# The attention of a chunk queued one slot later, from the fifth chunk on, in a linear-attention kernel followed by a gated feed-forward block

## The chip, the cores and the metric

The kernel runs on one core of a Trainium2 chip. The metric is device time in microseconds (us) of one execution, the median of several. Engines are named as in the profile: PE (TensorE, with its weight loads PEld), DVE (VectorE), ACT (ScalarE), POOL (GpSimd) and SP (the queue that issues most of the transfers).

## The reference

Queries, keys and values have shape (8 batches, 8 heads, 576 positions, 64), and `omega` maps 64 to 128 features. The result of the attention, 4608 tokens of 512 numbers, goes through two products that are multiplied element by element, and two more products.

```python
def phi(x):
    proj = np.einsum('bhsd,md->bhsm', x, omega)
    h = proj - np.sum(x * x, axis=-1, keepdims=True) / 2.0
    h = h - np.max(h, axis=-1, keepdims=True)
    return np.exp(h) / np.sqrt(m)
q_p, k_p = (phi(q * scale), phi(k * scale))
kv = np.einsum('bhsm,bhsd->bhmd', k_p, v)
z = np.sum(k_p, axis=2)
num = np.einsum('bhsm,bhmd->bhsd', q_p, kv)
den = np.einsum('bhsm,bhm->bhs', q_p, z)[..., None] + 1e-06
x = (num / den)          # then as 4608 x 512
a, b = x @ w1, x @ w2
out = (a * b @ w3) @ w_out
```

## The kernel before, in words

The tokens are cut into 36 chunks of 128, all heads together. A batch is 4.5 chunks long, so some chunks hold rows of two batches. Nearly every product is done in float16 with each operand split into a high and a low part, three matmuls in place of one (`PASSES`); a split costs one instruction for the high part and one for the low part, on two engines as the letters `KS`, `QS`, `VS`, `EH`, `EL`, `QH`, `QL` say.

What is done for one chunk of queries `c`, and where:

- `load`: SP fetches `qraw` and `kraw` (two buffers each).
- `norm` and `scale`: ACT sums squares (L153), PE adds them over partitions (`norm_q_k`, L158), DVE makes scales of them (L168 to L227).
- `split_raw`: ACT (L136) and DVE (L139) make `qhl`, `khl`; then the load of the chunk after next is issued.
- `features`: 24 PE matmuls into a PSUM tile `qpj` (or `kpj` for keys; L254); DVE finds the row maximum `nm` (L259) and subtracts it, `qe` (L267); ACT takes the exponential (L268).
- `q_chunk` (L337 on): after `features`, DVE casts the high part `eq` (L125), POOL makes the low part (L277), and SP issues two transposing transfers `eqT<-eq` (L344). `eqT` has two buffers, `eq` has one.
- `k_chunk` runs five chunks ahead (`LEAD`), with `ek` in place of `eq` and no transposition. When the last chunk of a batch has its `ek`, `kv_batch` runs 120 matmuls into `kvp` (L322), which ACT and DVE evict (L331, L332).
- Values: once for a batch, PE adds squares (`norm_v`), then POOL makes five high parts `vhl` (L138) and DVE five low parts (L139). These are called batch-of-values work below.
- `q_attend` (L346 on): 24 matmuls into a PSUM tile `nu` (L357; 48 of half the height where a chunk holds two batches), then DVE divides: `gd`, `gr`, `xs`, `mx` (L366 to L379).
- `ready`, with `x_turn` in it: DVE and ACT split the result, `xhl` (L393, L394), SP transposes it into `xT` (L398), and the units of the feed-forward block that need it are put in a queue.

The feed-forward units are `gate` (48 matmuls of 256 columns for a pair of chunks, L581, or 96 of 128 columns for each of the first four chunks; ACT, DVE and POOL turn them into two halves of `h`) and `project_out` (24 matmuls of 512 columns, L607; ACT scales it, L611, SP stores it). Each `project_out` also has a small DVE instruction `osc` (L603), whose four buffers come free when the ACT instruction of four units before is done. Three units belong to each chunk: two of `gate`, one of `project_out`.

Two PSUM pools matter. `ps_a` has two buffers of two banks, and `qpj`, `kpj`, `nu` and `kvp` take them in turn, in the order in which the Python code asks for them (function `banks`). `ps_m` has four buffers of one bank for everything else.

The order of the work comes from numbered slots. `step(i)` puts the parts of chunk `i` into slots with `put(slot, rank, fn)`; a chunk begins every three slots, at `at0`. At the end of the program one loop goes through the slots. In each slot it runs first a share of the work on the weights, then at most one unit of the feed-forward queue (above slot 40, `EAGER`, only if the queue holds more than two, `RESERVE`), then the parts put into the slot by rank, then one piece of work on values. Within that order a list scheduler places the instructions on each engine: an instruction that cannot start yet by its estimate lets later ones pass. Each engine runs its own list in order. Chunk `i` has its query and key features in slot `at0` (ranks 1 and 2), and before the change its attention in `at0 + 2` and `ready` in `at0 + 3`.

The weights (stored in 64 bits) are converted in the first 240 us or so, while the first chunks go through; this stretch is not repeated.

Of the kernel before, what the change touches and what calls it, by code (L numbers as in the profile page):

```python
# [47 lines left out]
GROUPS = [(0, 1), (1, 1), (2, 1), (3, 1)]  # L48
RESERVE = 2
EAGER = 40  # L50
RAW64_BUFS = 3
O_BUFS = 3
RAW_BUFS = 2
# [10 lines left out]
def tile_favor_attention_then_bilinear_ffn(  # L64
# [42 lines left out]
    def banks(name):  # L107
        return ps_a.tile([P, 2, 512], F32, tag="pa", name=name)
# [4 lines left out]
    def small(name, n=1, rows=P, dt=F32, bufs=4):  # L113
        return sm.tile([rows, n], dt, tag=f"s_{name}", name=name, bufs=bufs)
# [126 lines left out]
    def place(h):  # L241

        return h % 2 * NP + h // 2
# [102 lines left out]
    def q_attend(c):  # L346

        t = eqs.pop(c)
        owners = [
            (b, max(b * S - c * P, 0), min((b + 1) * S - c * P, P))  # L350
            for b in range(c * P // S, ((c + 1) * P - 1) // S + 1)
        ]
        nu = banks(f"nu_{c}")[:, :, 0 : 4 * E].rearrange("p g (i e) -> p g i e", e=E)
        for h in range(H):
            for b, r0, r1 in owners:
                for n, (x, y) in enumerate(PASSES):
                    nc.tensor.matmul(  # L357
                        nu[r0:r1, h // 4, h % 4],
                        t[:, x, place(h), r0:r1],
                        kvs[b][:, y, h],  # L360
                        start=n == 0,
                        stop=n == 2,
                    )

        gd = small("gd", H)
        nc.vector.tensor_scalar_add(  # L366
            gd.rearrange("p (g i) -> p g i", g=2), nu[:, :, :, D], 1e-6 * M * 2.0**21
        )
        gr = small("gr", H)
        nc.vector.reciprocal(gr, gd)  # L370
        xs = at.tile([P, HD], F32, tag="xs", name=f"xs_{c}", bufs=1)
        nc.vector.tensor_tensor(
            xs.rearrange("p (g i d) -> p g i d", g=2, d=D),
            nu[:, :, :, 0:D],
            gr.rearrange("p (g i) -> p g i", g=2).unsqueeze(3).broadcast_to([P, 2, 4, D]),
            ALU.mult,
        )
        mx = small("mx")
        nc.vector.tensor_reduce(mx, xs, AX.X, ALU.max, apply_absolute_value=True)  # L379
        xss[c] = xs, mx, owners  # L380

    def x_turn(c):

        xs, mx, owners = xss.pop(c)
        nc.vector.tensor_scalar(mx, mx, TINY, 2.0**-12, ALU.max, ALU.mult)
        p, r = pow2(mx, 1, f"x{c}")

        pt = sm.tile([P, 1], F32, tag="pt", name=f"pt_{c}", bufs=14)
        for b, r0, r1 in owners:
            nc.vector.tensor_scalar(pt[r0:r1], p[r0:r1], pv[b][r0:r1], None, ALU.mult)  # L390
        pts[c] = pt
        t = at.tile([P, 2, HD], F16, tag="xhl", name=f"xhl_{c}", bufs=1)
        nc.scalar.mul(t[:, 0], xs, r)  # L393
        nc.vector.scalar_tensor_tensor(t[:, 1], xs, r, t[:, 0], ALU.mult, ALU.subtract)  # L394
        mc, off = c * P // TOK, c * P % TOK
        if mc not in xT:
            xT[mc] = at.tile([P, 2, NC, TOK], F16, tag="xT", name=f"xT_{mc}", bufs=XT_BUFS)
        nc.sync.dma_start_transpose(  # L398
            xT[mc].rearrange("p x c s -> p (x c) s")[:, :, off : off + P],
            t.rearrange("p x d -> p (x d)"),  # L400
        )
# [16 lines left out]
    arena = const.tile([P, ARENA, 512], F32, name="arena")  # L418
    raw_at = list(range(0, 4 * RAW64_BUFS, 4))
    mag_at = list(range(4 * RAW64_BUFS, 4 * RAW64_BUFS + 4, 2))  # L420
    free = list(range(4 * RAW64_BUFS + 4, ARENA))

# [145 lines left out]
    def gate(c0, n, u):  # L568

        nf, T = 4 // n, n * P  # L570
        x = xT[c0 * P // TOK]
        off = c0 * P % TOK
        ab = []
        for m in range(2):
            ps = bank_m(f"ab_{c0}_{u}_{m}").rearrange("p (f s) -> p f s", f=nf)
            for k in range(nf):
                f = u * nf + k
                i, r = f // (NF // 2), f % (NF // 2)
                mm = [(cc, a, b) for cc in range(NC) for a, b in PASSES]
                for j, (cc, a, b) in enumerate(mm):  # L580
                    nc.tensor.matmul(  # L581
                        ps[:, k],
                        w12[m][i][cc][:, a, r * P : (r + 1) * P],
                        x[:, b, cc, off : off + T],
                        start=j == 0,
                        stop=j == len(mm) - 1,
                    )
            ab.append(ps)
        asb = mo.tile([P, nf, T], F32, tag="asb", name=f"asb_{c0}_{u}", bufs=ASB_BUFS)
        nc.scalar.mul(asb, ab[0], 2.0**-37)  # L590
        nc.vector.tensor_tensor(asb, ab[1], asb, ALU.mult)  # L591
        place = block()
        left[place] = nf * n
        h = arena[:, place].bitcast(F16).rearrange("p (x f s) -> p x f s", x=2, f=nf)
        nc.gpsimd.tensor_scalar(h[:, 0], asb, 1.0, 1.0, ALU.mult, ALU.mult)  # L595
        nc.gpsimd.tensor_tensor(h[:, 1], asb, h[:, 0], ALU.subtract)  # L596
        for k in range(nf):
            for t in range(n):
                hs[c0 + t, u * nf + k] = h[:, :, k, t * P : (t + 1) * P], place

    def project_out(c):
        sc = small("osc")
        nc.vector.tensor_scalar(sc, pts[c], pts[c], kap, ALU.mult, ALU.mult)  # L603
        ps = bank_m(f"o_{c}")
        mm = [(f, a, b) for f in range(NF) for a, b in PASSES]
        for i, (f, a, b) in enumerate(mm):
            nc.tensor.matmul(ps, hs[c, f][0][:, a], W[f][:, b], start=i == 0, stop=i == len(mm) - 1)  # L607
        for f in range(NF):
            used(hs[c, f][1])
        o = mo.tile([P, DO], F32, tag="o", name=f"o_{c}", bufs=O_BUFS)  # L610
        nc.scalar.mul(o, ps, sc)  # L611
        nc.sync.dma_start(out[c * P : (c + 1) * P, :], o)
# [15 lines left out]
    def v_unit(n=1):  # L628
        for x in v_work[:n]:
            x()  # L630
        del v_work[:n]
# [51 lines left out]
    def put(slot, rank, fn):  # L683
        plan.setdefault(slot, []).append((rank, len(plan[slot]) if slot in plan else 0, fn))
# [3 lines left out]
    def ready(c):  # L688
        x_turn(c)
        for c0, m in groups:  # L690
            if c0 + m == c + 1:
                units = []
                for u in range(2 * m):
                    need = [(n, u // m) for n in range(2)]
                    units.append((need, lambda c0=c0, m=m, u=u: gate(c0, m, u)))

                for k, f in enumerate(behind_by):
                    units.insert(2 + 3 * k, f)
                behind_by[:] = [(["k"], lambda c=c: project_out(c)) for c in range(c0, c0 + m)]
                queue.extend(units)  # L700
                if c + 1 == NCH:
                    queue.extend(behind_by)

    def step(i):
        at0 = begin[i]
        kc = i + LEAD
        keys = [(n, c) for n, c in (("q", i), ("k", kc)) if 0 <= c < NCH]
        state = {}

        def norms():  # L710
            state["am"] = norm(keys, i)

        def splits():
            for name, c in keys:
                split_raw(c, name)
                if c + 2 < NCH:
                    load(srcs[name], c + 2, name)

        put(at0 - 3, 3, norms)
        put(at0 - 2, 6, lambda: scale(keys, state["am"]))  # L720
        put(at0 - 1, 8, splits)
        if i >= 0:
            put(at0, 1, lambda: q_chunk(i))
            put(at0 + 2, 7, lambda: q_attend(i))
            put(at0 + 3, 0, lambda: ready(i))
        if kc < NCH:
            put(at0, 2, lambda: k_chunk(kc))
        if kc in B_OF_K:

            def kv():  # L730
                v_unit(len(v_work))
                kv_batch(B_OF_K[kc])

            put((begin[i + 1] if i + 1 in begin else at0 + 3) - 1, 5, kv)
        for b in range(B):
            cs = [c for c, _, _ in chunks_of(b)]
            if cs[1] == kc:
                put(at0, 9, lambda b=b: v_batch(b))
            if cs[0] == kc:
                put(at0 + 2, 10, lambda cs=cs: [v_load(c) for c in cs if c not in vraw])  # L740
# [7 lines left out]
    for t in range(max(plan) + 1):  # L748
        n = min(PER[t] if t < len(PER) else 1, len(ticks))
        weights(n)  # L750
        if not ticks and raw_at:
            for a, w in [(a, 4) for a in raw_at] + [(a, 2) for a in mag_at]:
                free.extend(range(a, a + w))
            raw_at.clear()
        unit(RESERVE if t > EAGER else 0)
        for _, _, fn in sorted(plan.get(t, []), key=lambda x: x[:2]):
# [43 lines left out]
```

## Time and profile before

| | |
|---|---|
| median of 3 runs | 932.87 us (929.71 to 1192.34) |
| the profiled execution, its own time | 932.87 us |
| its span in the trace | 931.1 us |
| PE busy | 809.9 us, 87% |
| PEld / DVE / ACT / POOL busy | 64% / 68% / 44% / 35% |
| waits of PE at `nu` for the transposed features `eqT`, 312 to 876 us | 26.3 us in 15 waits |

How to read it: the span is covered by PE for 87%, so a microsecond taken from another engine shows in the time only where PE waits for it. One run of the three shown is far above the others, and the median is the run that was profiled. The 1.8 us between the span and the time lie around the span.

In the rows of the timeline the columns are: start, length, engine, line, operation, tile written and tiles read, matmul shape, count, and in brackets the idle time of the engine before it and what ended it.

### The profile page before, as it was taken

The page shows a single profiled execution, that of the slowest core. Times are in us where ns is not written, and L with a number is a line of the kernel's source. Part 1 is how long each engine was busy: PE and PEld are TensorE (multiplying, and loading weights), DVE is VectorE, ACT ScalarE, POOL GpSimd, SP SyncE. Part 2 cuts the span into 40 slices and gives each one's busy share as a digit, 9 for nine tenths or more (in the row PEclk, how much of TensorE's full clock was granted, in tenths as well). Part 3 has the DMA queues.
Part 4 walks back from the last instruction along what each step waited for, and adds up shares of the span by engine and source line. Part 5 has one row for each costly group of instructions (what it writes and reads, how often), then busy time and mean ns, then how long its engine had stood idle before and what let it go on. Part 6 is the DMA issues. An engine that isn't in the chain of part 4 may idle for free.

```text
span 931.1 us, 20482 instructions
## 1 busy us (share of the span) xinstructions
PE 809.9 (87%) x8593; PEld 598.3 (64%) x8598; DVE 637.7 (68%) x1119; ACT 406.9 (44%) x695; POOL 324.7 (35%) x317
## 2 busy tenths in 40 slices
PE   1964397689996998999989998989899989999998
PEld 1433253577775766777757766767577757777774
DVE  5779789889787478667876787566857875556210
ACT  3587764556435343444344533444354333322111
POOL 0000004232454256433543464343533643423311
PEclk9985599689998799999989998999899989999999
DMA  8445455332444145333432343243423422333200
GB/s 312 163 137 181 136 148 178 83 70 59 92 114 83 43 91 126 92 70 81 114 80 69 80 125 80 65 96 79 115 71 69 69 59 58 74 76 58 46 24 34
DMA packets 142524, 88.42 MB, mean 95 GB/s; under 512 B 116704, under 2 KB 116832, under 8 KB 142432
## 3 DMA queue, kind: packets, MB, share of 16 engines
q1 hardware_dynamic: 134944, 66.15, 30.1%
q10 hardware_dynamic: 7488, 20.97, 6.7%
q8 instruction: 67, 1.10, 0.5%
q14 instruction: 25, 0.20, 0.1%
HBM read 49.35 MB, written 9.44 MB: 63 GB/s over the span
## 4 chain that ended last, share of the span: by engine, by line
PE 45%; DVE 25%; ACT 11%; DMA 10%; issue 5%; POOL 4%; ACTq 0%; DVEq 0%; SPq 0%; another core or an unknown queue 0%; POOLq 0%
PE ab L581 24%; PE o L607 9%; DVE nm L259 5%; PE kvp L322 4%; PE wp L530 4%; DMA eqT<-eq 3%; DMA qraw<-qT 3%; DVE qhl L139 3%; DVE vhl L139 2%; DVE qe L267 2%; POOL eq L277 2%; PE nu L357 2%; DVE ke L267 2%; ACT ke L268 1%; DMA xT<-xhl 1%
## 5 line engine op out<-in xcount | busy, mean ns | idle before, releaser
L581 PE MATMUL ab<-xT,w12b 128*128 128x256 f16 (+1 forms) x3840 | 408.7, 268 | 12.8 <-DMA xT<-xhl 11.4
L581 PEld LDWEIGHTS <-w12b 128*128 128x128 f16 x3840 | 351.4, 101 | 59.4 <-DMA xT<-xhl 6.8
L607 PE MATMUL o<-Wb,arena 128*128 128x512 f16 x864 | 194.4, 379 | 1.3 <-DVE Wb L139 0.8
L595 POOL TENSOR_SCALAR arena<-asb 128x512 f16<-128x512 f32 x72 | 59.7, 829 | 256.4 <-DVE asb L591 249.5
L607 PEld LDWEIGHTS <-arena 128*128 128x128 f16 x864 | 84.4, 100 | 93.9 <-issue 1.4
L277 POOL TENSOR_TENSOR eq<-qe,eq 128x1024 f16<-128x1024 f32 x34 | 73.3, 2157 | 139.7 <-DVE eq L125 139.7
L268 ACT ACTIVATE qe<-qe,ln_e,es 128x1024 f32<-128x1024 f32 x35 | 43.4, 1240 | 149.5 <-DVE qe L267 149.5
L596 POOL TENSOR_TENSOR arena<-asb,arena 128x512 f16<-128x512 f32 x72 | 92.0, 1277 | 6.0
L139 DVE SCALAR_TENSOR_TENSOR qhl<-qraw,s,qhl 128x512 f16<-128x512 f32 x36 | 68.5, 1904 | 28.6 <-ACT qhl L136 28.5
L591 DVE TENSOR_TENSOR asb<-ab,asb 128x512 f32<-128x512 f32 x72 | 49.5, 688 | 55.3 <-PE ab L581 54.9
L277 POOL TENSOR_TENSOR ek<-ke,ek 128x1024 f16<-128x1024 f32 x28 | 61.5, 2195 | 46.6 <-DVE ek L125 45.3
L153 ACT ACTIVATE junk_q<-qraw 128x512 bf16<-128x512 f32 x36 | 22.7, 631 | 125.2 <-DMA qraw<-qT 125.2
L357 PE MATMUL nu<-kv,eqT 128*128 128x65 f16 (+1 forms) x960 | 40.7, 204 | 40.5 <-DMA eqT<-eq 40.0
L357 PEld LDWEIGHTS <-eqT 128*128 128x128 f16 (+1 forms) x960 | 35.6, 107 | 51.6 <-DMA eqT<-eq 45.2
L530 PE MATMUL wp<-w12b 128*128 128x512 f32 x128 | 62.4, 644 | 4.8 <-DVE w12b L461 4.8
L322 PE MATMUL kvp<-vhl,ek 128*128 128x65 f16 x960 | 50.5, 206 | 11.0 <-POOL ek L277 4.7
L603 DVE TENSOR_SCALAR osc<-pt,kap 128x1 f32<-128x1 f32 x36 | 9.6, 272 | 68.8 <-ACT o L611 68.7
L322 PEld LDWEIGHTS <-ek 128*128 128x128 f16 x960 | 41.4, 104 | 22.4 <-POOL ek L277 4.8
L590 ACT ACTIVATE asb<-ab 128x512 f32<-128x512 f32 x72 | 41.8, 580 | 28.2 <-PE ab L581 28.2
L254 PE MATMUL kpj<-om,khl 64*128 64x128 f16 x864 | 34.0, 226 | 21.5 <-ACT khl L136 17.2
L530 PEld LDWEIGHTS wp<-w12b 128*128 128x128 f32 x128 | 25.7, 206 | 35.6 <-issue 29.9
L393 ACT ACTIVATE xhl<-xs,p2r 128x512 f16<-128x512 f32 x36 | 25.8, 718 | 49.3 <-DVE p2r L182 44.3
(120 smaller groups left out, 1037.5 us busy)
## 6 DMA issues: line engine op xcount, KB each, us to landing
kraw<-kT SPq DMA_DIRECT2D x36, 256.0 KB, 3.0
vraw<-v SPq DMA_DIRECT2D x36, 256.0 KB, 3.0
qraw<-qT SPq DMA_DIRECT2D x36, 256.0 KB, 2.6
out<-o SPq DMA_DIRECT2D x36, 256.0 KB, 2.0
arena<-w3T ACTq DMA_DIRECT2D x8, 1024.0 KB, 5.4
arena<-w ACTq DMA_DIRECT2D x8, 1024.0 KB, 5.9
arena<-wo ACTq DMA_DIRECT2D x4, 1024.0 KB, 5.3
eqT<-eq SPq DMA_TRANSPOSE x72, 3.0
```

What stands on the lines that cost most here:

```text
L139: nc.vector.scalar_tensor_tensor(lo, src, s, hi, ALU.mult, ALU.subtract)
L259: nc.vector.tensor_reduce(nm, pj, AX.X, ALU.max, negate=True)
L268: nc.scalar.activation(e, e, AF.Exp, scale=es, bias=ln_e)
L277: (nc.vector if lo == "d" else nc.gpsimd).tensor_tensor(t[:, 1], e, t[:, 0], ALU.subtract)
L322: nc.tensor.matmul(ps[:, h // 4, h % 4], ek[c][r0:r1, x, place(h)], vhl[c][r0:r1, y, h], start=n == 0, stop=n == len(mm) - 1,)
L357: nc.tensor.matmul(nu[r0:r1, h // 4, h % 4], t[:, x, place(h), r0:r1], kvs[b][:, y, h], start=n == 0, stop=n == 2,)
L530: nc.tensor.matmul(ps, w[:, j, k * P : (k + 1) * P], guest[:, j], start=j == 0, stop=j == HALF - 1)
L581: nc.tensor.matmul(ps[:, k], w12[m][i][cc][:, a, r * P : (r + 1) * P], x[:, b, cc, off : off + T], start=j == 0, stop=j == len(mm) - 1,)
L591: nc.vector.tensor_tensor(asb, ab[1], asb, ALU.mult)
L595: nc.gpsimd.tensor_scalar(h[:, 0], asb, 1.0, 1.0, ALU.mult, ALU.mult)
L596: nc.gpsimd.tensor_tensor(h[:, 1], asb, h[:, 0], ALU.subtract)
L607: nc.tensor.matmul(ps, hs[c, f][0][:, a], W[f][:, b], start=i == 0, stop=i == len(mm) - 1)
```

## The change

A constant `EARLY = 4`, and in `step` a lag of 2 slots for the first four chunks and of 3 for all others. Both the attention and what follows it (`ready`) move by one slot.

```diff
 EAGER = 40
+EARLY = 4
 RAW64_BUFS = 3
...
         if i >= 0:
             put(at0, 1, lambda: q_chunk(i))
-            put(at0 + 2, 7, lambda: q_attend(i))
-            put(at0 + 3, 0, lambda: ready(i))
+            lag = 2 if i < EARLY else 3
+            put(at0 + lag, 7, lambda: q_attend(i))
+            put(at0 + lag + 1, 0, lambda: ready(i))
```

Since a chunk has three slots, a lag of 3 puts the attention of chunk `i` into the slot in which chunk `i + 1` begins, behind its query and key features (ranks 1 and 2 against 7). The line numbers behind the inserted lines are higher by one, and by two at the end of the program. No instruction of arithmetic is added or taken away.

The first place is PE in the steady part of the program, around the attention of chunk 20. In the names, the first number behind a tile is the chunk (for `ab` the first chunk of the pair, the unit and the factor). Before:

```order
L254 MATMUL qpj_20_7253<-om_82,qhl_20_7167 128x128
...
L254 MATMUL kpj_25_7289<-om_82,khl_25_7172 128x128
...
L581 MATMUL ab_16_3_0_7328<-xT_8_6261,w12b_104 128x256
...
L607 MATMUL o_15_7398<-Wb_105,arena_107 128x512
...
L357 MATMUL nu_20_7426<-kv_4_6439,eqT_20_7286 128x65
...
L581 MATMUL ab_18_0_0_7474<-xT_9_6962,w12b_104 128x256
...
L254 MATMUL qpj_21_7541<-om_82,qhl_21_7459 128x128
```

And with the change:

```order
L608 MATMUL o_15_7413<-Wb_105,arena_107 128x512
...
L255 MATMUL qpj_21_7441<-om_82,qhl_21_7396 128x128
...
L255 MATMUL kpj_26_7477<-om_82,khl_26_7401 128x128
...
L582 MATMUL ab_18_0_0_7552<-xT_9_7037,w12b_104 128x256
...
L358 MATMUL nu_20_7514<-kv_4_6409,eqT_20_7187 128x65
...
L582 MATMUL ab_18_0_1_7577<-xT_9_7037,w12b_104 128x256
```

Before, the attention of chunk 20 stands between a projection and a gate, 24 `qpj`, 24 `kpj`, 48 `ab` and 24 `o` matmuls behind the first `qpj` of its own chunk. Now it stands behind `qpj` and `kpj` of the next chunks, with 10 matmuls of the following gate between; the other 38 of that gate half come after it.

The second place is DVE, where the values of a batch are split (`vhl`), around the same chunk. Before:

```order
L139 SCALAR_TENSOR_TENSOR vhl_25_7614<-vraw_25_6610,s1_3_7183,vhl_25_7614 128x8x64
L591 TENSOR_TENSOR asb_16_2_7237<-ab_16_2_1_7212,asb_16_2_7237 128x512
L139 SCALAR_TENSOR_TENSOR vhl_26_7682<-vraw_26_6612,s1_3_7183,vhl_26_7682 128x8x64
L259 TENSOR_REDUCE nm_7278<-qpj_20_7253 128x8
L267 TENSOR_TENSOR qe_20_7280<-qpj_20_7253,nm_7278 128x1024
L259 TENSOR_REDUCE nm_7314<-kpj_25_7289 128x8
L267 TENSOR_TENSOR ke_25_7316<-kpj_25_7289,nm_7314 128x1024
L125 CAST eq_20_7283<-qe_20_7280 128x1024
```

And with the change:

```order
L140 SCALAR_TENSOR_TENSOR vhl_25_7547<-vraw_25_6547,s1_3_7120,vhl_25_7547 128x8x64
L140 SCALAR_TENSOR_TENSOR vhl_26_7627<-vraw_26_6549,s1_3_7120,vhl_26_7627 128x8x64
L604 TENSOR_SCALAR osc_8415<-pt_18_7032,kap_106 128x1
L260 TENSOR_REDUCE nm_7179<-qpj_20_7154 128x8
L268 TENSOR_TENSOR qe_20_7181<-qpj_20_7154,nm_7179 128x1024
L260 TENSOR_REDUCE nm_7215<-kpj_25_7190 128x8
L367 TENSOR_SCALAR gd_7252<-nu_19_7227 128x8
L126 CAST eq_20_7184<-qe_20_7181 128x1024
```

The split of the values still stands ahead of `nm` and `qe` of chunk 20. What is new is that `gd`, the first step behind the attention of chunk 19, follows them directly, and that `osc` stands ahead of `nm`.

## The prediction

> **What bounds the kernel now.** I read the page first, then the waits of PE, then PE's timeline period by period.
>
> ```profile
> span 931.1 us, 20482 instructions
> PE 809.9 (87%) x8593; PEld 598.3 (64%) x8598; DVE 637.7 (68%) x1119; ACT 406.9 (44%) x695; POOL 324.7 (35%) x317
> ```
>
> PE is busy for 87%, so what counts is where PE waits. In the window from 312 to 876 us its waits have one line:
>
> ```profile
> PE nu L357 <- DMA eqT<-eq: 26.3, 15, 2.7
> ```
>
> All is waiting of the attention for the transposed query features, which the change addresses. What a quiet period looks like, and what a bad one, shows in PE's timeline:
>
> ```profile
> 507.74 0.84 PE L254 MATMUL qpj<-om,qhl 64*128 64x128 f16 x24
> 508.42 0.83 PE L254 MATMUL kpj<-om,khl 64*128 64x128 f16 x24
> 509.18 5.41 PE L581 MATMUL ab<-xT,w12b 128*128 128x256 f16 x48
> 514.43 0.28 PE L158 MATMUL norm_q_k<-sums,ones 128*128 128x3 f32 x2
> 514.58 5.34 PE L607 MATMUL o<-Wb,arena 128*128 128x512 f16 x24
> 519.75 0.90 PE L357 MATMUL nu<-kv,eqT 128*128 128x65 f16 x24
> 520.49 5.40 PE L581 MATMUL ab<-xT,w12b 128*128 128x256 f16 x48
> 525.83 0.84 PE L254 MATMUL qpj<-om,qhl 64*128 64x128 f16 x24
> ```
>
> From `qpj` to the next `qpj` are 525.83 - 507.74 = 18.09 us, and no row waits: the least that PE can do per chunk. A chunk with the values of a batch:
>
> ```profile
> 459.02 0.84 PE L254 MATMUL qpj<-om,qhl 64*128 64x128 f16 x24
> ...
> 473.68 0.24 PE L357 MATMUL nu<-kv,eqT 128*128 128x65 f16 x2 [2.48 <-DMA eqT<-eq]
> 475.85 1.39 PE L357 MATMUL nu<-kv,eqT 128*128 128x65 f16 x22 [1.94 <-DMA eqT<-eq]
> 477.06 7.35 PE L581 MATMUL ab<-xT,w12b 128*128 128x256 f16 x48
> ...
> 484.34 0.84 PE L254 MATMUL qpj<-om,qhl 64*128 64x128 f16 x24
> ```
>
> 484.34 - 459.02 = 25.32 us, 7.23 more than the quiet one: 4.42 of waiting and, behind it, matmuls at a lower clock (22 of `nu` in 1.39 instead of about 0.85, the gate half in 7.35 instead of 5.40, 2.5 together). The period behind it, with the 120 `kvp` matmuls, takes 507.74 - 484.34 = 23.40 us, so `kvp` is worth 5.31.
>
> **The change part by part.** *What is removed.* The steady stretch runs from the `qpj` of chunk 9 to that of chunk 31:
>
> ```profile
> 319.00 0.84 PE L254 MATMUL qpj<-om,qhl 64*128 64x128 f16 x24
> ...
> 787.59 0.84 PE L254 MATMUL qpj<-om,qhl 64*128 64x128 f16 x24
> ```
>
> That is 468.6 us for 22 periods. Without waits they would take 22 x 18.09 = 398.0, plus five `kvp` at 5.31 = 26.6, plus some 1.5 for `norm_v` and for the two chunks with two batches: 426.1. The loss is 42.5 us: 26.3 of waiting and about 16 of cold clock. With the attention a slot later, the transfers started a whole period earlier, and this loss goes completely. I take -42.5.
>
> *What is added.* The order of PE puts `nu` of chunk i behind `qpj` of chunk i+1. `ps_a` has two buffers and both are handed out in turn, so `nu` gets the buffer of the `qpj` two requests before, and cannot start until DVE has read that `qpj` for the last time, in `qe`. Before, the `qe` in question was a slot and a half back and cost nothing. Now it is the one that just began. No row of before shows this wait; its length follows from the rows of DVE beside the quiet period:
>
> ```profile
> 508.62 1.23 DVE L259 TENSOR_REDUCE nm<-qpj 128x8 f32<-128x1024 f32 x1
> 509.95 1.23 DVE L267 TENSOR_TENSOR qe<-qpj,nm 128x1024 f32<-128x1024 f32 x1
> ```
>
> `nm` starts 0.88 behind the start of `qpj` (507.74), and `qe` ends at 511.18, 3.44 behind it. PE meanwhile has `kpj` and the 10 matmuls that the order leaves ahead of `nu`: 509.18 - 507.74 = 1.44, and 10 of 48 matmuls of a gate half of 5.25 = 1.09, together 2.53. The wait is 0.9. One more thing stands ahead of `nm`: `osc`, which waits for the ACT instruction of the projection that ends just ahead of `qpj`. From the end of the program, where nothing else is in the way:
>
> ```profile
> 869.01 0.90 PE L357 MATMUL nu<-kv,eqT 128*128 128x65 f16 x24
> ...
> 869.21 0.69 ACT L611 ACTIVATE o<-o,osc 128x512 f32<-128x512 f32 x1 [6.28 <-PE o L607]
> 869.93 0.27 DVE L603 TENSOR_SCALAR osc<-pt,kap 128x1 f32<-128x1 f32 x1 [5.14 <-ACT o L611]
> ```
>
> ACT starts 0.20 after the next PE work, `osc` at 0.92, so `nm` at about 1.1 instead of 0.88. I take 1.2 us of wait in a chunk without values; 0.9 is the lower bound, 1.5 the upper.
>
> In a chunk with values, `vhl` stands ahead of `nm` on DVE. Before:
>
> ```profile
> 458.02 4.66 POOL L138 TENSOR_SCALAR vhl<-vraw,s 128x512 f16<-128x512 f32 x5 [3.69 <-DVE pv L303]
> ...
> 464.41 0.74 DVE L139 SCALAR_TENSOR_TENSOR vhl<-vraw,s,vhl 64x512 f16<-64x512 f32 x1
> 465.07 1.21 DVE L259 TENSOR_REDUCE nm<-qpj 128x8 f32<-128x1024 f32 x1
> ```
>
> `nm` started 465.07 - 459.02 = 6.05 after its `qpj`, against 0.88: this is what made `eqT` late there. With the change `norm_v` and `vhl` stand behind the second gate half of a period. Counting from `qpj`: the wait ends at 3.7, `nu` 4.5, 38 gate matmuls to 8.6, norm 8.8, the second half to 14.0, `norm_v`, then 24 `o` to 19.6, the next `qpj`. DVE evicts the second half by about 15.6 (its splits `qhl` and `khl` end near 15), has the scale of the values by 16.4, and POOL, which has the half's `h` first, works on it:
>
> ```profile
> L595 POOL TENSOR_SCALAR arena<-asb 128x512 f16<-128x512 f32 x72 | 59.7, 829 | 256.4 <-DVE asb L591 249.5
> L596 POOL TENSOR_TENSOR arena<-asb,arena 128x512 f16<-128x512 f32 x72 | 92.0, 1277 | 6.0
> ```
>
> 0.83 + 1.28 takes it to 17.7, five `vhl` at 4.66 to 22.4, the last of DVE to 23.1, so `nm` at 23.2 instead of 19.6 + 1.1 = 20.7: 2.5 more, a wait of 3.7. A wait of that length costs clock too; I take 2.3, a little under the 2.5 above. Together 6.0 for each of the five. Bounds: 1.2 (POOL and DVE are done in time) to 8 (two more us on POOL). Sum: 17 x 1.2 + 5 x 6.0 = 20.4 + 30 = +50.4.
>
> [...]
>
> ```profile
> 612.67 0.84 PE L254 MATMUL qpj<-om,qhl 64*128 64x128 f16 x24
> ...
> 627.34 1.03 PE L357 MATMUL nu<-kv,eqT 128*128 128x65 f16 x22 [2.42 <-DMA eqT<-eq]
> 628.18 6.89 PE L581 MATMUL ab<-xT,w12b 128*128 128x256 f16 x48
> 635.01 0.84 PE L254 MATMUL qpj<-om,qhl 64*128 64x128 f16 x24
> ```
>
> Here one wait of 2.42 was enough: the period took 22.34, 4.25 too much, of which 1.8 is clock.
>
> *What moves beside it.* The results of the attention (`xs`, `xhl`, the transfer `xT`) come a slot later, behind `eqT` of the next chunk on SP, and `ready` too. The gates that need them come a slot later in the same measure, so a unit has the same distance to its input; the transfer hides behind the three units of stock. POOL's list only exchanges `vhl` and one pair of `h`; that is in the sum. From chunk 31 on there are no keys: `nu` gets the other buffer, and nothing waits there, as now. The last units are the same in both orders: 0.
>
> *The start of the steady part*, 205 to 319 us. The queue is empty at slots 41 and 42 before, and for one slot more with the change, and the attention of chunk 5 comes ahead of fewer units, so the first gate of a pair will wait for it, some 5 us. Against this, two waits are there now:
>
> ```profile
> 284.46 0.29 PE L357 MATMUL nu<-kv,eqT 128*128 128x65 f16 x2 [4.34 <-DMA eqT<-eq]
> 304.73 7.57 PE L322 MATMUL kvp<-vhl,ek 64*128 64x65 f16 x106 [4.68 <-POOL ek L277]
> ```
>
> With their clock (106 `kvp` in 7.57 where 120 take 5.31 warm, 2.9) about 14 us. Bounds -14 (both go, nothing comes) to +8 (both stay in another form and one gateless slot of 5 to 8 is added); I take -3, nearer to nothing, since both come from a pipeline that is short of finished chunks, which the change does not alter.
>
> **Sum**: -42.5 + 50.4 - 3 = +4.9 us. The profiled execution's time is 932.87, also the median shown, so 937.8.
>
> **The rivals.**
>
> *It does not matter either way (932).* What the transfers lose now, the buffers lose then, to within a few us, or the parts of the start decide. For it: the two numbers of the sum are close because both come from the same DVE work ahead of `nm`.
>
> *The buffer is free in time (908).* If POOL and DVE finish the values ahead of the next `qpj`, all 22 waits are about 1: 932.87 - 42.5 + 22 x 1.0 - 3 = 909, and 908 at 0.95. For it: DVE is busy for only 68%. Against: `vhl` needs POOL for 4.66 us behind a `norm_v` that has not moved ahead.
>
> *The short waits chill PE (968).* If a wait of 1.2 already lowers the clock, 17 of them cost the 1.8 of the row at 627.34 as well: 937.8 + 17 x 1.8 = 968. The point from which it decides lies somewhere below 2.42 us of wait. For it: PE is then interrupted in every chunk, not in every fourth. Against: the trace has a wait of 1.94 only together with one of 2.48, and small waits in quiet periods left the clock alone. [...]
>
> **How the numbers follow.** Forecast 0.52, no matter 0.15, free in time 0.14, chilled 0.19. Within 2% (914.2 to 951.5, about what a measurement of this kernel can tell from no change) lie the second and nearly all of the first. The likeliest is 938. Its own range is 921 to 953: 16 us up or down, from 1.2 to 8 for the values and -14 to +8 at the start, which will not all fall on one side. Its top end lies beyond 951.5; I count 0.04 of the 0.52 there. So faster 0.14, slower 0.19 + 0.04 = 0.23, same 0.63. The range reaches into the two outer cases until 2 in 10 are left out: 910 to 962.
>
> **What would show it.** Right: no wait of `nu` for `eqT` behind 320 us, but one for DVE `qe` in nearly every chunk, about 1.2 us, and five of 3 to 4 us with slow matmuls behind them; a quiet period of 19.3 instead of 18.09; periods with values near 24. Wrong: quiet periods still at 18.1 (then `nu` does not wait for that buffer), or all at 19.3 with none above 21 (free in time), or gate halves of 6 us and more in quiet periods (chilled).

## The result, and the profile after

| | before | with the change |
|---|---|---|
| median of 4 runs | 932.31 us | 945.8 us (943.15 to 946.97) |
| ratio to before | | 1.015, 95% interval 1.0116 to 1.0184 |
| profiled execution: time, span | 932.87, 931.1 us | 946.97, 945.2 us |
| `qpj` of chunk 9 to that of chunk 31 | 468.6 us | 478.5 us |
| ahead of it / behind it | 319.0 / 143.5 us | 317.6 / 149.1 us |

One of the four executions of before took 1192.34 us; the ratios here and below leave such slow executions out.

The kernel became 1.5% slower. That is less than the 2% of the forecast's classes, but clear of the noise, and inside the stated range, 7.8 us above the predicted 938.

The page's first lines of the change, and PE's waits in the steady part and behind it (waiting line, what was waited for, us in total, times, longest):

```profile
span 945.2 us, 20461 instructions
...
PE 810.0 (86%) x8593; PEld 596.9 (63%) x8598; DVE 626.4 (66%) x1119; ACT 410.2 (43%) x695; POOL 312.1 (33%) x317
```

```profile
PE nu L358 <- DVE qe L268: 35.7, 21, 4.1
PE nu L358 <- DMA vraw<-v: 3.7, 1, 3.7
```

PE does the same work in 810.0 us. All waiting for `eqT` is gone; in its place `nu` waits for `qe` in every chunk that still has keys. The second row is the same wait: the profile names what ended last ahead of it by its events, here a load of values that has nothing to do with `nu`, while `qe` ended 0.15 us ahead of `nu` (468.07 + 1.23 = 469.30 against 469.45 below).

PE's timeline of the change, a quiet period:

```profile
513.40 0.84 PE L255 MATMUL qpj<-om,qhl 64*128 64x128 f16 x24
...
514.85 1.26 PE L582 MATMUL ab<-xT,w12b 128*128 128x256 f16 x10
517.11 0.89 PE L358 MATMUL nu<-kv,eqT 128*128 128x65 f16 x24 [0.99 <-DVE qe L268]
517.84 4.31 PE L582 MATMUL ab<-xT,w12b 128*128 128x256 f16 x38
...
532.64 0.84 PE L255 MATMUL qpj<-om,qhl 64*128 64x128 f16 x24
```

and DVE beside it:

```profile
514.23 0.27 DVE L604 TENSOR_SCALAR osc<-pt,kap 128x1 f32<-128x1 f32 x1 [4.22 <-ACT o L612]
514.42 1.22 DVE L260 TENSOR_REDUCE nm<-qpj 128x8 f32<-128x1024 f32 x1
515.74 1.23 DVE L268 TENSOR_TENSOR qe<-qpj,nm 128x1024 f32<-128x1024 f32 x1
```

The period is 532.64 - 513.40 = 19.24 us, 1.15 more than the 18.09 of before. `nm` starts 1.02 behind its `qpj`, right behind `osc`; `qe` ends 3.57 behind it, and `nu` can start. PE has run out of work at 2.7. The 38 gate matmuls behind the wait take 4.31, as behind the other waits of 0.99, and the granted clock is 1.00 from 512 to 524 us: this wait of 0.99 us did not touch it.

A chunk with values, PE and DVE together:

```profile
461.60 5.13 DVE L140 SCALAR_TENSOR_TENSOR vhl<-vraw,s,vhl 128x512 f16<-128x512 f32 x5 [1.93 <-POOL vhl L139]
...
463.00 0.84 PE L255 MATMUL qpj<-om,qhl 64*128 64x128 f16 x24
...
466.65 0.26 DVE L604 TENSOR_SCALAR osc<-pt,kap 128x1 f32<-128x1 f32 x1
466.83 1.20 DVE L260 TENSOR_REDUCE nm<-qpj 128x8 f32<-128x1024 f32 x1
468.07 1.23 DVE L268 TENSOR_TENSOR qe<-qpj,nm 128x1024 f32<-128x1024 f32 x1
...
469.45 1.48 PE L358 MATMUL nu<-kv,eqT 128*128 128x65 f16 x24 [3.74 <-DMA vraw<-v]
470.74 6.49 PE L582 MATMUL ab<-xT,w12b 128*128 128x256 f16 x38
...
487.72 0.84 PE L255 MATMUL qpj<-om,qhl 64*128 64x128 f16 x24
```

Five low parts `vhl` fill DVE until 466.7, `nm` starts 3.83 behind its `qpj` in place of 1.02, and PE waits for 3.74 us. Behind it the same 38 matmuls take 6.49. The period is 24.72 us.

### The profile page after: what moved, and what is told of

Its sections match the earlier page's. It is cut to its first block, busy times and chain, and to the rows that moved or that the text cites. A ratio compares the mean times of both kernels' runs of the same rounds, so it can differ in the third digit from the quotient of the medians.

```text
span 945.2 us, 20461 instructions
## 1 busy us (share of the span) xinstructions
PE 810.0 (86%) x8593; PEld 596.9 (63%) x8598; DVE 626.4 (66%) x1119; ACT 410.2 (43%) x695; POOL 312.1 (33%) x317
## 4 chain that ended last, share of the span: by engine, by line
PE 52%; DVE 25%; ACT 10%; issue 5%; DMA 5%; POOL 2%; ACTq 0%; SPq 0%; DVEq 0%; POOLq 0%
PE ab L582 27%; PE o L608 14%; PE kvp L323 5%; DVE nm L260 4%; PE wp L531 3%; DVE qe L268 3%; DVE vhl L140 3%; PE nu L358 2%; DVE xhl L395 2%; DMA kraw<-kT 1%; DVE ke L268 1%; ACT ke L266 1%; ACT o L612 1%; DVE arena L461 1%; ACT qe L269 1%
## 5 line engine op out<-in xcount | busy, mean ns | idle before, releaser
L596 POOL TENSOR_SCALAR arena<-asb 128x512 f16<-128x512 f32 x72 | 56.4, 783 | 141.6 <-DVE asb L592 119.2
L597 POOL TENSOR_TENSOR arena<-asb,arena 128x512 f16<-128x512 f32 x72 | 83.5, 1160 | 6.0
L358 PE MATMUL nu<-kv,eqT 128*128 128x65 f16 (+1 forms) x960 | 36.4, 201 | 49.1 <-DVE qe L268 36.8
L358 PEld LDWEIGHTS <-eqT 128*128 128x128 f16 (+1 forms) x960 | 32.7, 105 | 57.5 <-issue 30.9
L395 DVE SCALAR_TENSOR_TENSOR xhl<-xs,p2r,xhl 128x512 f16<-128x512 f32 x36 | 62.0, 1723 | 9.9 <-ACT xhl L394 9.4
L531 PE MATMUL wp<-w12b 128*128 128x512 f32 x128 | 60.4, 627 | 4.9 <-DVE w12b L462 4.9
L612 ACT ACTIVATE o<-o,osc 128x512 f32<-128x512 f32 x36 | 24.6, 683 | 90.9 <-PE o L608 90.8
L137 ACT ACTIVATE qhl<-qraw,s 128x512 f16<-128x512 f32 x36 | 25.9, 721 | 78.8 <-DVE s L174 76.8
L255 PE MATMUL kpj<-om,khl 64*128 64x128 f16 x864 | 36.0, 231 | 21.8 <-ACT khl L137 17.5
```

Of the source, the lines that this page charges most:

```text
L358: nc.tensor.matmul(nu[r0:r1, h // 4, h % 4], t[:, x, place(h), r0:r1], kvs[b][:, y, h], start=n == 0, stop=n == 2,)
L531: nc.tensor.matmul(ps, w[:, j, k * P : (k + 1) * P], guest[:, j], start=j == 0, stop=j == HALF - 1)
```

## The experiments

The theory from the prediction has two halves. What the change **removes** is waiting for `eqT`, which is late because DVE's list is held up in the chunks with values. What it **adds** is a wait of `nu` for a PSUM buffer, which is free once `qe` has read the `qpj` of the next chunk, and is therefore as long as DVE's list is late there too. The main rival is that it is the lag itself: a later attention costs, whatever buffer it has. The times, each beside runs of the kernel before on the same chip:

| kernel | edit | median, us | before there | ratio, 95% interval |
|---|---|---|---|---|
| lag_four | lag 4 | 900.7 | 934.2 | 0.965 (0.960 to 0.970) |
| attend_first | lag 3, attention ahead of the features | 950.2 | 934.2 | 1.019 (1.013 to 1.025) |
| third_pair_lag3 | lag 3, three buffers in `ps_a`, two in `ps_m` | 995.3 | 933.6 | 1.067 (1.063 to 1.071) |
| values_on_act_lag3 | lag 3, high parts of values by ACT | 935.3 | 934.2 | 1.002 (0.999 to 1.006) |
| values_on_act_lag2 | before, high parts of values by ACT | 923.2 | 934.2 | 0.988 (0.985 to 0.992) |
| values_low_on_pool | lag 3, values split on POOL and ACT | 958.3 | 933.6 | 1.026 (1.020 to 1.032) |
| values_on_pool_osc_free | the same, eight buffers for `osc` | 908.7 | 934.0 | 0.974 (0.971 to 0.977) |
| osc_free_lag3 | lag 3, eight buffers for `osc` | 940.5 | 933.4 | 1.007 (1.004 to 1.010) |
| osc_free_lag2 | before, eight buffers for `osc` | 910.3 | 933.4 | 0.976 (0.971 to 0.981) |
| lag_three_from_nine | lag 3 from the tenth chunk on | 944.7 | 933.6 | 1.013 (1.009 to 1.017) |
| lag_four_values_on_pool | lag 4, values on POOL and ACT | 891.3 | 933.6 | 0.955 (0.951 to 0.959) |
| lag_four_all | the same, eight buffers for `osc` | 889.1 | 934.0 | 0.953 (0.950 to 0.956) |

### Is it the lag? A lag of four

```diff
-            lag = 2 if i < EARLY else 3
+            lag = 2 if i < EARLY else 4
```

> Lag of 4 slots in place of 3 from the fifth chunk on; on PE the attention nu of chunk i then stands behind qpj and kpj of the next chunks AND a whole projection o (24 matmuls), 6.9 us behind that qpj. Theory (nu waits only because it is given the PSUM buffer of the qpj just ahead, which qe frees 3.6 us later, 6.3 us in chunks with values): no wait of nu is left in either kind of chunk, the steady stretch falls from 478.5 us to about 426, and the time from 946 to about 895 (up to 903 if the start loses one more gateless slot). Rival one (what limits is how far the finished chunks are ahead of the gates, so each further slot costs): gates wait for xT in most chunks, 935 or more. Rival two (PE waits for whatever DVE is late with, whichever tile): waits of about the same sum at other lines, 940 to 950.

It ran in 900.7 us. PE's timeline of this kernel, a quiet period:

```profile
386.17 0.84 PE L255 MATMUL qpj<-om,qhl 64*128 64x128 f16 x24
...
387.62 5.36 PE L608 MATMUL o<-Wb,arena 128*128 128x512 f16 x24
...
392.95 0.89 PE L358 MATMUL nu<-kv,eqT 128*128 128x65 f16 x24
393.68 10.65 PE L582 MATMUL ab<-xT,w12b 128*128 128x256 f16 x96
404.25 0.84 PE L255 MATMUL qpj<-om,qhl 64*128 64x128 f16 x24
```

18.08 us without a wait. One slot more of lag makes the kernel faster by 45 us, so the lag as such is not what costs: `nu` now stands a whole projection behind the `qpj` whose buffer it takes, and the buffer is free by then. Rival one is refuted, and rival two as well: behind 240 us `nu` waits for 11.0 us in all, in place of 40.3, and no other line of PE takes the rest over. `nu` still waits for `qe` by 0.5 to 1.7 us in and directly behind the chunks with values, which the theory had not expected: `qe` is later there than the 6.3 us reckoned. That the time fell into the expected range all the same is in part luck. The 21 periods from the `qpj` of chunk 10 to that of chunk 31 take 418.1 us, 10 more than without waits, while the stretch ahead of them came out 11.9 us shorter than in the change (325.1 against 337.0), and the end 5.2 longer.

### Is it the buffer? Another order of asking, and a third buffer

```diff
-            put(at0 + lag, 7, lambda: q_attend(i))
+            put(at0 + lag, 7 if i < EARLY else 0.5, lambda: q_attend(i))
```

> Lag 3 as in the change, but from the fifth chunk on the attention is queued ahead of the features of the next chunk in the same slot (rank 0.5 for 7). nu then asks for its buffer first and gets that of the qpj of its own chunk, read a period ago; kpj, two requests later, gets the buffer of nu. Theory (the buffer handed out decides who waits): nu waits for nothing, and kpj waits for xs, the last reader of nu: xs ends about 2.25 us behind the start of nu and PE is at kpj after 1.42, so 0.8 to 0.9 us in a normal chunk, and about 3.4 in each of the five with values: 17 x 0.85 + 5 x 5.5 = 42 on a stretch of 426, 468, and a time of about 935 (927 to 944). Rival (nu waits because it comes a slot later, whichever buffer it has): nu still waits for DVE qe, about 1 us a chunk, 946. Second rival (kpj has slack because the list scheduler lets gate matmuls pass): no wait anywhere, 900 to 910.

The largest line of PE's waits behind 240 us, and a quiet stretch of this kernel's timeline:

```profile
PE kpj L255 <- DVE xs L373: 35.8, 23, 4.5
```

```profile
408.57 0.90 PE L358 MATMUL nu<-kv,eqT 128*128 128x65 f16 x24
409.40 0.84 PE L255 MATMUL qpj<-om,qhl 64*128 64x128 f16 x24
410.94 0.85 PE L255 MATMUL kpj<-om,khl 64*128 64x128 f16 x24 [0.70 <-DVE xs L373]
```

The wait moved from `nu` to `kpj`, and its releaser from `qe` to `xs`, the last reader of `nu`: exactly the tile that gets the buffer waits, for exactly the instruction that frees it. Both rivals are refuted. The sum stayed near what it was, 35.8 us against 35.7 + 3.7, since DVE is as late as before (0.70 in a quiet chunk, but up to 4.5 where `vhl` stands ahead). The time, 950.2 against the 927 to 944 expected, missed: the waits with values were a microsecond longer than reckoned, and the start took 322.9 us to the `qpj` of chunk 9.

```diff
-    ps_a = ctx.enter_context(tc.tile_pool(name="ps_a", bufs=2, space=PSUM))
-    ps_m = ctx.enter_context(tc.tile_pool(name="ps_m", bufs=4, space=PSUM))
+    ps_a = ctx.enter_context(tc.tile_pool(name="ps_a", bufs=3, space=PSUM))
+    ps_m = ctx.enter_context(tc.tile_pool(name="ps_m", bufs=2, space=PSUM))
```

> The change with three buffers in ps_a and, to pay for the two banks, two in place of four in ps_m. nu, qpj and kpj then each keep a buffer of their own, and nu gets the one of the attention before. Theory (the wait of nu is the buffer that two requests earlier went to the qpj just ahead): no wait of nu for DVE qe is left in any chunk, normal or with values, though nu now stands directly behind kpj. What two buffers in ps_m cost is not known from any run: waits of ab, norm or o that were not there, so the time lies between 895 (they cost nothing) and 950. Rival (nu has to wait for DVE in that place, whatever its buffer): waits of nu of 2 us and more a chunk, since 10 gate matmuls less stand ahead of it, and 960 or more.

The two largest lines of PE's waits behind 240 us, and `nu` in its timeline:

```profile
PE ab L582 <- DVE asb L592: 35.3, 22, 3.9
PE norm_q_k L159 <- ACT asb L591: 15.1, 19, 2.4
```

```profile
533.32 0.91 PE L358 MATMUL nu<-kv,eqT 128*128 128x65 f16 x24
534.07 5.41 PE L582 MATMUL ab<-xT,w12b 128*128 128x256 f16 x48
...
541.39 5.40 PE L582 MATMUL ab<-xT,w12b 128*128 128x256 f16 x48 [1.30 <-DVE asb L592]
```

With a buffer of its own `nu` waits for nothing, 1.4 us behind the start of `qpj` and with no gate matmul between: its place in the order was never the cause. The two banks taken from the gates cost more than they bring, 50.4 us of waits for their eviction, and the time is 995.3, beyond the 950 given as an upper bound.

### What makes DVE late in the chunks with values

```diff
-VS = "aaaaam"
+VS = "a"
```

> The change, with the high parts of the values made by ACT instead of POOL (VS all a). Theory (in the five chunks with values nu waits 3.7 to 4.1 us because vhl on POOL starts late, behind a pair of h, and takes 4.65 us, so that nm is 2.8 us late on DVE): ACT has its five done some 2 us earlier, nm starts nearly on time, the five periods fall from about 24.1 to 19.3 to 20.5 us and the time from 946 to 922 to 930. Rival (it is the five low parts on DVE, or the scale of the values, whoever makes the high parts): the five waits stay above 3 us, 943 to 948. The waits of 1.0 us in the other chunks stay in both cases.

> The kernel before (lag 2 everywhere), with the high parts of the values made by ACT instead of POOL. Theory (there too vhl on POOL ahead of nm is what makes eqT late in the five chunks with values): nm starts some 2.6 us earlier, the waits of 4.4 us shrink to 1.5 to 2.5, the clock falls less, 932 becomes 908 to 920. Rival (the wait is for other DVE work or for the transposing transfer itself): five waits of 4 us and more stay, 928 to 936.

With lag 3 the time was 935.3, above the 922 to 930 expected, and the five waits only fell to between 2.4 and 3.4 us (3.40, 2.99, 3.27, 3.09 and 2.38; the expectation for `values_low_on_pool` below says 3.0 to 3.4). ACT, DVE and PE of that kernel:

```profile
451.94 3.16 ACT L137 ACTIVATE vhl<-vraw,s 128x512 f16<-128x512 f32 x5
452.69 3.40 DVE L140 SCALAR_TENSOR_TENSOR vhl<-vraw,s,vhl 128x512 f16<-128x512 f32 x5 [2.83 <-ACT vhl L137]
453.17 0.84 PE L255 MATMUL qpj<-om,qhl 64*128 64x128 f16 x24
...
455.01 0.67 ACT L612 ACTIVATE o<-o,osc 128x512 f32<-128x512 f32 x1
456.00 0.26 DVE L604 TENSOR_SCALAR osc<-pt,kap 128x1 f32<-128x1 f32 x1
456.19 1.20 DVE L260 TENSOR_REDUCE nm<-qpj 128x8 f32<-128x1024 f32 x1
```

`nm` starts 3.02 behind its `qpj` in place of 3.83, though ACT needs 3.16 us and not POOL's 4.65. Two things ate the rest: ACT starts only at 451.94, behind sums of squares, and the five low parts still fill DVE for 3.40 us, until 456.09. `osc` follows them without a pause; the `o` that it needs ended at 455.68, so it is not `osc` that waits here. The theory that POOL is the cause was too narrow. In the profiled execution the steady stretch is 6.7 us shorter (471.8 in place of 478.5), and the stretch ahead of it 9.1 (308.5 in place of 317.6).

With lag 2 the time was 923.2, above the 908 to 920 expected and below the rival's 928 to 936. `nm` came 5.37 behind its `qpj` in place of 6.05, but the list scheduler put the `nm` of the keys ahead of `qe`, so `qe` started 7.64 behind it in place of 7.29. The waits for `eqT` fell only from 26.3 to 23.4 us in all, and the five with values to between 3.0 and 4.1. This run decides nothing about the wait. Its profiled execution took 926.07 us, 6.8 less than that of before; 4.5 of them lie in the steady stretch and 2.2 ahead of it.

```diff
-VS = "aaaaam"
+VS = "aaaaap"
```

> The change, with the values of a batch split on POOL and ACT alone (POOL scales, ACT makes the high part, POOL the low part), so that no low part of the values stands ahead of nm on DVE. Moving only the high parts to ACT brought the five waits from 3.7 to 4.1 us down to 3.0 to 3.4. Theory (what delays nm there is the row of five vhl instructions in DVE's list, whoever feeds it): nm starts 1.0 us behind its qpj as in the other chunks, the five waits become 1.0, the five periods 19.2 to 19.4 in place of 23.6 to 24.8, and the time falls by about 24 us, 946 to 922 (918 to 928). Rival (nm is late for something else there, osc or the scale of the values, or POOL's 10 us of extra work delays eq and h): five waits above 2.5 us, 935 or more. The waits of 1.0 in the other 17 chunks stay.

The time rose to 958.3, in place of the 918 to 928 expected. ACT, DVE and PE of this kernel:

```profile
460.76 0.62 ACT L128 CAST vhl<-vraw 64x512 f16<-64x512 f32 x1 [1.11 <-POOL vraw L142]
461.28 0.68 ACT L612 ACTIVATE o<-o,osc 128x512 f32<-128x512 f32 x1
461.99 0.27 DVE L604 TENSOR_SCALAR osc<-pt,kap 128x1 f32<-128x1 f32 x1 [9.08 <-ACT o L612]
462.18 1.21 DVE L260 TENSOR_REDUCE nm<-qpj 128x8 f32<-128x1024 f32 x1
...
464.87 1.48 PE L358 MATMUL nu<-kv,eqT 128*128 128x65 f16 x24 [5.91 <-DMA vraw<-v]
```

No `vhl` stands in DVE's list, and still `nm` starts 5.93 us behind its `qpj` (at 456.25), in place of 3.83 in the change. DVE is idle for 9.08 us in front of `osc`, one instruction of 0.27 us: it writes a buffer that ACT's `o` of four units before must have read, that `o` stands in ACT's list behind five casts, and these wait for POOL. The work had gone from DVE, the wait had not. The rival as written, `osc`, was right. The next two runs take the wait away by giving it buffers:

```diff
-        sc = small("osc")
+        sc = small("osc", bufs=8)
```

> The change with the values split on POOL and ACT, and eight buffers for osc in place of four. With the values on POOL alone the five waits had grown to 5.9 to 6.7 us: the trace shows DVE idle for 9.08 us in front of osc, which waits for the ACT instruction of a projection, which stands in ACT's list behind the casts of the values, which wait for POOL. nm and qe stand behind osc. Theory (the wait of nu is as long as qe is late, whatever holds DVE's list up: vhl in the change, osc there): with eight buffers osc waits for nothing, nm starts right behind its qpj, the five waits fall to 0.8 to 1.0 and so do those of the other chunks from 1.0 to about 0.85, and the time is 918 to 925. Rival (the values hold the chunk up in another way, through POOL or the transposed features): five waits above 2.5 us stay, 935 or more.

> The change with eight buffers for osc in place of four and nothing else. Theory (osc costs 0.12 us a chunk where nothing else holds DVE up, as the waits of 0.88 in place of 1.0 showed, and in the chunks with values vhl ends just ahead of osc, so there osc costs only its own 0.2): the waits of nu go from 1.0 to 0.88 and from 3.7 to 4.1 to about 3.5, the time from 946 to 941 to 944. Rival (osc was the main cause in the chunks with values, and vhl none): the five waits fall to about 1, 920.

With both edits PE's waits behind 240 us have one line for `nu`, and a chunk with values looks like any other:

```profile
PE nu L358 <- DVE qe L268: 20.5, 23, 1.2
```

```profile
449.58 0.84 PE L255 MATMUL qpj<-om,qhl 64*128 64x128 f16 x24
...
453.17 0.89 PE L358 MATMUL nu<-kv,eqT 128*128 128x65 f16 x24 [0.87 <-DVE qe L268]
```

The steady stretch falls from 478.5 to 448.7, 29.8 us, and that is what the theory gives: 25 from the five chunks with values, and 5 from the others, whose waits are now 0.9, but for one of 1.2. The time, 908.7, is 9 below the expected range, because the start was 7.7 us shorter as well (310.0 against 317.6). This is the kernel that the rival "the buffer is free in time" had described, and its price of 908 was right, by its own terms too: the steady stretch is 19.9 us shorter than before (21.6 in the rival's sum), the start and the end together 3.5 us (3 in its sum). With `osc` free alone the normal waits fell to 0.88 and the five stayed at 3.5 to 3.9 us: there `vhl` is the cause, and each of the two hides the other. Its 940.5 lie half a microsecond below what was expected.

> The kernel before with eight buffers for osc and nothing else. In its chunks with values DVE stood idle for 2.02 us in front of osc, and the scale of the values stands behind osc, then vhl, then nm. Theory (the wait of 4.4 us for eqT there is the lateness of this one list, whatever causes it): scale, vhl and nm come about 2 us earlier, the five waits fall from about 4.4 to 2 to 2.5 and their cold clock with them, 933 to 910 to 920. Rival (the transposing transfers or POOL set that wait): it stays, 930 to 936.

This is the same edit in the kernel before, and it alone made it faster by 2.4%, 910.3 us. In the chunk with values of before, DVE stood idle in front of `osc`, with the scale of the values behind it:

```profile
456.25 0.27 DVE L603 TENSOR_SCALAR osc<-pt,kap 128x1 f32<-128x1 f32 x1 [2.02 <-ACT o L611]
```

With eight buffers, PE and DVE around the same chunk:

```profile
452.77 0.84 PE L254 MATMUL qpj<-om,qhl 64*128 64x128 f16 x24
...
457.01 1.20 DVE L259 TENSOR_REDUCE nm<-qpj 128x8 f32<-128x1024 f32 x1
...
465.27 0.24 PE L357 MATMUL nu<-kv,eqT 128*128 128x65 f16 x2 [0.32 <-DMA eqT<-eq]
467.47 1.39 PE L357 MATMUL nu<-kv,eqT 128*128 128x65 f16 x22 [1.96 <-DMA eqT<-eq]
```

`nm` starts 4.24 behind its `qpj` in place of 6.05, and the waits are 2.28 in place of 4.42, as forecast (1.9 to 2.8 in the five). So the waits that the change was aimed at hang on the same list of DVE as the waits that it brought.

### The start, and all together

```diff
-EARLY = 4
+EARLY = 9
```

> The change, but from the tenth chunk on (EARLY = 9) in place of the fifth. The traces show that the stretch before the qpj of chunk 9 took 319.0 us before and 317.6 after, though one unit of about 5.4 us had moved from it to the end of the program, so the start itself lost about 4. Theory (the start loses by the longer lag while finished chunks are scarce): with the start as it was before the time is 3 to 5 us less than that of the change, 941 to 944. Rival (the start is as short of chunks with the one lag as with the other and its stalls only fall elsewhere): no difference, 945 to 948.

944.7 us against 945.8, with overlapping intervals: nothing is decided by the time. In the profiles the stretch up to the `qpj` of chunk 9 is 4.5 us shorter than in the change once the unit of 5.35 us that moved is counted (318.5 against 317.6 + 5.35), so the start did lose something. But the profiled executions differ by 3.3 us and the medians by 1.1, so the size of this term stays open. The stalls themselves follow the lag: with the first nine chunks at a lag of 2 those of before are back, 4.34 us for `eqT` and 3.91 for `ek`, and of the two waits for `qhl` in the change (7.3 us, shown further below) 0.5 us is left.

> A lag of 4 from the fifth chunk on and the values split on POOL and ACT alone. With the lag of 4 alone the time was 900.7 and nu still waited 1.0 to 1.7 us for qe in the five chunks with values and once or twice behind them. Theory (these are the same five vhl on DVE): no wait of nu is left from the tenth chunk on, 10 to 15 us less of waits and what follows from them, 888 to 894. Rival (POOL becomes the late one: its 10 us of extra work delay ek and with it kvp, or h and with it o): new waits at kvp or o, 900 or more.

> All that helped together: a lag of 4, the values split on POOL and ACT, eight buffers for osc. With the first two the time was 891.3, and 3.4 us of waits of nu were left in all, none of them in the steady part. Theory (behind 300 us nothing waits any more, what is left is the work of PE and the start): 886 to 892, no difference that counts. Rival (osc still delays qe or the attention of a chunk with values): 880 to 885.

891.3 and 889.1 us. In the second, the 21 periods from the `qpj` of chunk 10 to that of chunk 31 take 410.2 us, against 426.1 - 18.09 = 408.0 for a stretch without waits: no wait worth removing is left there. It is 4.7% faster than before, and the fastest kernel of the study. `osc` brought nothing clear on top (2.3 us, on another chip), as expected: without it `nu` had a single wait of 0.36 us left between the `qpj` of chunk 10 and that of chunk 31.

## Why the prediction came out as it did

| term, us | predicted | measured |
|---|---|---|
| waits for `eqT` and their clock go | -42.5 | -42.5, as reckoned |
| 17 chunks without values | +20.4 | +22.1 |
| five chunks with values | +30 | +30.3 |
| start, and the last units | -3 | +4.2 |
| sum, on the profiled execution | +4.9 | +14.1 |

- **What is removed**: right. No wait for `eqT` is left, and the stretch without waits, reckoned as 426.1, was reached within 2.2 us by the best kernel. The measured column takes the 42.5 over from it and puts the remainder into the two rows below, which are uncertain by as much.
- **The buffer**: right, shown by three runs: the wait moves with the order of asking, goes with a third buffer, and goes, in the chunks away from the values, when more work of PE stands ahead of it.
- **Its length**: 1.2 predicted, 1.0 measured, and the period 1.15 longer; `nm` was forecast at 1.1 behind `qpj` and came at 1.02. The row of 17 is a little dearer because two of them stand behind a chunk with values (2.12 and 2.01 us of wait) and two hold two batches (1.38 and 1.36).
- **The chunks with values**: 3.7 predicted, 3.7 to 4.1 measured, with 1.95 of clock each (30.3 less 19.8 of waits and 0.15 for each interrupted gate, over five) against 2.3. Single chunks lie between 1.3 and 2.7, so that the mean came so close is in part luck: with the five waits the clock stayed at half for 3.41 or for 6.83 us, as the last section shows. The cause given, the POOL work, was only part of it: the run of five low parts in DVE's list is what delays `nm`, and `osc` is ready to take its place.
- **Start and end**: this is the term that was mis-sized, by 7.2 us, most of the miss. "The last units are the same in both orders: 0" counted instructions and not the stretch they fall into: the end got 5.6 us longer, because one unit of the feed-forward block moved behind the `qpj` of chunk 31. The stretch ahead of chunk 9 lost that unit and should have been shorter by it, 313.7; it took 317.6. The unit that moved cancels between the two, so the step that failed is the start: put at 3 us of gain, it lost about 4 for the same work. The two stalls counted as gains there came back in another form, as PE's timeline of the change shows:

```profile
265.79 0.28 PE L255 MATMUL qpj<-om,qhl 64*128 64x128 f16 x4 [3.54 <-ACT qhl L137]
...
292.32 0.40 PE L255 MATMUL qpj<-om,qhl 64*128 64x128 f16 x4 [3.76 <-ACT qhl L137]
```

  Ahead of the first, PE's order has nothing between `norm_q_k` (261.97) and this `qpj`, where before two gate halves and an attention stood (260.34 to 271.87). DVE finishes the scale that `qhl` needs only behind the `xhl` of the attention, which ends at 264.89. So the slot without a gate that the prediction had in its upper bound came, as a wait of `qpj` and not of a gate for `xT`. That is read from the rows; no run tries it apart. The bounds of -14 to +8 held the term.
- **The rivals**: "the short waits chill PE" is refuted, waits of 1.0 left the gate halves at 1.26 + 4.31, and between 320 and 800 us the granted clock falls five times only, each time in a chunk with values. "It does not matter either way" missed by 14 us, and by its reason: the two sums did not cancel. "The buffer is free in time" does not describe this change, but a kernel two edits away.

## What to carry to other kernels

Where the stall went when work was queued later depended here on who got the buffers (35.7 us at `nu` in the change, 35.8 at `kpj` with the other order of asking): list the requests of a rotating pool in order, and for each tile find the last reader of the one that had its buffer before. A tiny instruction in a list that runs in order can be the longest wait of all (9.08 us in front of the 0.27 of `osc`); look at the idle time in front of it before moving the large instructions behind it. And if one step of a shift only exchanges one wait for another, try the next step: one slot more was worth 45 us here.

## What the runs showed of the hardware

The clock did not follow the length of a wait. In the change, the granted clock (third column from the end: share of full speed, a mean over the 2 us of the row) around the wait at 469.45:

```profile
468.00:470.00 2.00, 0.55 (x11) 0.58 (x12) 1.97 (x3) 0.61 (x1) 0.00 (x0) 0.60 0.59 217
470.00:472.00 2.00, 2.00 (x23) 1.60 (x21) 1.46 (x4) 0.64 (x1) 0.15 (x1) 0.50 0.00 0
...
474.00:476.00 2.00, 2.00 (x15) 1.52 (x14) 1.03 (x5) 1.96 (x3) 0.00 (x0) 0.70 0.58 113
```

Seen in steps of 0.2 us it is 1.00 until 468.38 and 0.50 until 475.21, so here it stays at half for 6.83 us, 5.8 of them after PE is back at work. But a wait of 3.55 us left it untouched, as the 38 matmuls behind it show in the change with `osc` free:

```profile
466.24 0.90 PE L358 MATMUL nu<-kv,eqT 128*128 128x65 f16 x24 [3.55 <-DVE qe L268]
466.97 4.32 PE L582 MATMUL ab<-xT,w12b 128*128 128x256 f16 x38
```

while the one of 2.42 us in the prediction's rows lowered it, to 0.50 from 627.83 to 631.24, for 3.41 us. So there is no length of the wait from which the clock falls in all these rows, as the prediction supposed somewhere below 2.42 us; what sets the wait of 3.55 apart was not shown.

In the change, from 320 to 800 us, the clock stayed at 1.00 with all waits of 0.88 to 2.12 us. It fell to 0.50 once with each of the five of 3.73 to 4.11 us, for 3.41 us with those of 3.73 and 4.11 (two of this length), and for 6.83 us with those of 3.74 and 4.10. So even among these the clock lost does not grow with the wait.
